# One written order of instructions replaced by another in a fused linear-attention and gated feed-forward kernel

## The chip, the cores and the metric

The kernel runs on one core of a Trainium2 chip. The metric is the device time of one execution in microseconds (us). The core has five engines that run side by side, each working through its own list of instructions in order: TensorE (PE, matrix products), VectorE (DVE), ScalarE (ACT), GpSimd (POOL) and SyncE (SP, which here only issues transfers by DMA). They wait for each other through semaphores.

## The reference

```python
q_s = exp(q - max(q, -1)); q_s /= sum(q_s, -1) + 1e-9      # softmax over the 64 head features
k_s = exp(k - max(k, 2));  k_s /= sum(k_s, 2) + 1e-9       # softmax over the 576 positions
kv  = einsum('bhsd,bhse->bhde', k_s, v)                    # one 64x64 matrix per head
x   = einsum('bhsd,bhde->bhse', q_s, kv)                   # 8 batches, 8 heads, 576 positions
x   = x.transpose(0, 2, 1, 3).reshape(4608, 512)
h   = x @ w_in                                             # 512 -> 2048
out = (h / (1 + exp(-beta * h))) @ w_out                   # 2048 -> 512, float32
```

All inputs and the output are float32; matrix operands are bfloat16 in the kernel.

## The kernel before, in words

The 4608 tokens are worked in nine chunks of 512: chunks 0 to 6 and 8 are the first 512 tokens of batches 0 to 7, and chunk 7 collects the last 64 tokens of every batch (`TAILS`). Each chunk goes through 16 steps `u`, one for every 128 of the 2048 hidden features. Steps are numbered through, `n = 16 * chunk + u`, 144 in all.

- `h n` (`st1`, L861): four matmuls of 512 columns, one for each of four contraction tiles, make `h` in one of four PSUM banks (`hT`). For `n` below 4 a step is cut into halves of 256 tokens and again into two parts of two contraction tiles (`h n half part`).
- `th n` (`tanh`, L879, ACT): tanh of `beta * h`, read from the bank.
- `g n` (`gate`, L896, DVE): `(th + 1) * h`, in bfloat16, one of 12 buffers. It frees the bank. The factor one half is put into the kv matrices.
- `o n` (`st2`, L927, and L919 in the last chunk): four matmuls add the step to four PSUM accumulators (`acc`). `oev` copies an accumulator to SBUF after 16 steps, `st` stores it.

Ahead of a chunk, its batch goes through the attention. `qmax`, `qsub`, `qexp`, `qsum`, `qrcp`, `qnorm` make the softmax of q; `kmax`, `kred`, `ksmall`, `krep`, `ksub`, `kexp` that of k; `vcast` turns v into bfloat16; `kv` (L617) and `kvn` (L636 to L639) make the kv matrices; `qtr` with its copy `qtrev` (batches 0 and 1, on PE), or `qT` (later batches, a transposing DMA issued by SP, L442), turn q; `x` (L667) multiplies, and `xev` copies `x` to the buffer `xT` in bfloat16, from which `h` reads. `xt` and `xtev` do that for the last 64 tokens. In batch 0 the pieces are smaller: `xev b jp half` (`x_ev_half`) writes the contraction tiles `jp` and `jp + 2` for one half of the chunk's tokens, a strided write. `kswap 0` (L495) exchanges key maxima between partitions by a matmul; `beta tr` (L342) transposes beta.

Loads are `ld q`, `ld k`, `ld v` (two for each batch, 576 KB each), `ld w` (16 parts of the two weights, 512 KB each, into four staging buffers) and `ld beta`. `cast w` turns a part into bfloat16. Batch `b` loads into the buffer of batch `b - 2`, so a load can stand behind the work of that batch. Eight semaphores serve SP's transfers in turn, so a transfer is issued once the one eight places before it has landed. `fill` are matmuls on constants that give PE something to do in the head.

What sets the order is the text `ORDER` at the top of the file (L17): a list of 1212 operations, written out by hand or by a planner outside the file. The last lines of the kernel go through it and issue each operation's instructions, in that order, to its engine; a word after `=` names the engine of an operation that has a choice:

```python
with tc.manual_schedule():
    for name, _, e in plan:
        fn, eng = ops[name]
        eng = e or eng
        fn(ENGINES[eng]) if eng else fn()
```

No engine changes its order at run time. The four `hT` banks are dealt out by the order too (`take`: the bank that has been free for the longest in the list), and so are the transfer semaphores. Waits are derived from the tiles and the ranges in them that the instructions touch.

Of the kernel before, what the change touches and what calls it, by code (L numbers as in the profile page):

```python
# [42 lines left out]
h_16_1, g_17, qmax_2_1, ld_w7_0, ld_k2_0, cast_w7_0=act, th_16, g_16, ld_q3_0, ld_v2_1, h_18, h_19, th_20, kmax_2_1,
th_18, o_12, g_20, g_18, qsub_2_0=pool, kmax_2_0, th_19, kred_2, g_19, qexp_2_3, ld_w7_1, h_23, th_23, qexp_2_1,
h_22, qexp_2_2, o_13, h_21, g_23, h_24, cast_w7_1=pool, o_14, ksmall_2, o_15, qexp_2_0, krep_2, th_21, ksub_2_0=pool,
g_21, qsum_2_2, th_22, g_22, qsum_2_3, vcast_2_1=act, qsum_2_1, oev_0_2=dve, oev_0_1=act, h_25, th_24, ld_v3_1,
ld_k3_0, g_24, qrcp_2_1, oev_0_0=act, oev_0_3=act, h_26, th_26, h_27, th_25, g_25, o_16, h_28, ld_v2_0, h_29, o_17,
kexp_2_0, ld_q4_0, ld_q3_1, qmax_3_1, ksub_2_1=pool, g_26, kexp_2_2, qmax_3_2, kexp_2_1, qnorm_2_1=pool, qsum_2_0,
o_18, o_19, vcast_3_1=act, th_28, ld_k3_1, st_0_3, qrcp_2_0, g_28, th_27, g_27, o_20, th_29, ld_v4_1, g_29, kmax_3_0,
ld_q4_1, qmax_3_0, kexp_2_3, vcast_2_0=pool, kv_2_0, kv_2_1, xt_0, xtev_0_0=act, ld_k4_0, o_21, xtev_0_1=dve,  # L50
qnorm_2_0=pool, qsub_3_0=pool, o_22, qexp_3_1, h_31, th_31, h_30, qexp_3_0, th_30, qmax_3_3, kmax_3_1, kmax_3_3,
o_23, o_24, kvn_2, o_25, o_26, qsub_3_1=pool, g_31, qexp_3_2, kmax_3_2, g_30, kred_3, qsum_3_2, qT_2, x_2_0,
# [981 lines left out]
```

## Time and profile before

| | us |
|---|---|
| median of three runs | 288.36 (288.12 to 288.61) |
| the profiled execution | 289.07 |
| its span, first to last instruction | 287.3 |
| PE busy | 277.1 |
| DVE busy | 202.1 |
| ACT busy | 175.3 |
| POOL busy | 127.9 |

The page is of one execution and reads like this: a row of a timeline has the start, the length, the engine, the line, the instruction, what it writes and reads, the number of instructions merged into the row, and in brackets how long the engine had been idle and what ended that. A matmul's shown length is that of a pipelined instruction: four matmuls of 512 columns that follow each other take about 0.86 us, less than their lengths together. Idle time of an engine that does not set the pace costs nothing.

### The profile page before, as it was taken

To read this page: it belongs to the slowest core of one execution; us is meant where nothing else is said; L and a number is where in the kernel's file an instruction comes from. 1 tells how busy PE (TensorE), PEld (TensorE's weight loads), DVE (VectorE), ACT (ScalarE), POOL (GpSimd) and SP (SyncE) were. 2 spreads that over 40 slices of the span, in tenths; PEclk is the share of its full clock that TensorE was granted. 3 is DMA by queue.
4 is the path that set the end of the run, shared out by engine and by line. 5 is a ranking of instruction groups with operands and counts; after the bars stand their busy time and mean duration, and the time that the engine had idled before them with its cause. 6 is when DMAs were issued, how large, how long until landed. Compare 5 with 4: busy or idle time off the path is not lost.

```text
span 287.3 us, 5186 instructions
## 1 busy us (share of the span) xinstructions
PE 277.1 (96%) x1969; PEld 128.9 (45%) x1969; DVE 202.1 (70%) x413; ACT 175.3 (61%) x302; POOL 127.9 (45%) x90
## 2 busy tenths in 40 slices
PE   7689999999999999999999999999999999999994
PEld 3255444444444444444444444444444444444542
DVE  3889967999999889999888747544664354536330
ACT  4878795995779577666875446436643454334422
POOL 5699895588398993367963620430020000000000
PEclk9899999999999999999999999999999999999999
DMA  7999999888966899950032930800025003000404
GB/s 254 385 392 387 387 387 390 321 294 267 256 178 228 188 341 390 280 169 1 0 96 108 209 149 1 228 2 0 2 66 165 0 3 145 0 0 1 148 0 146
DMA packets 36808, 50.01 MB, mean 174 GB/s; under 512 B 15648, under 2 KB 15920, under 8 KB 36784
## 3 DMA queue, kind: packets, MB, share of 16 engines
q1 hardware_dynamic: 36640, 49.56, 52.7%
q8 instruction: 15, 0.25, 0.4%
q10 hardware_dynamic: 144, 0.13, 0.1%
...
## 4 chain that ended last, share of the span: by engine, by line
PE 85%; DVE 5%; DMA 3%; POOL 2%; ACT 1%; issue 1%; SPq 1%; ACTq 0%
PE acc L927 40%; PE hT L861 40%; DMA beta_rows<-in_moe_beta_dram 3%; POOL kf L543 2%; PE hT L617 2%; DVE g L896 1%; PE hT L667 1%; SPq L273 1%; DVE km L478 1%; DVE kf L543 1%; PE hT L919 1%; PE acc L919 1%; DVE qs L420 1%; ACT th L879 1%; ACT xT L230 1%
## 5 line engine op out<-in xcount | busy, mean ns | idle before, releaser
L879 ACT ACTIVATE th<-hT,beta_c 128x512 bf16<-128x512 f32 (+1 forms) x148 | 95.3, 676 | 72.8 <-PE hT L861 54.5
L896 DVE SCALAR_TENSOR_TENSOR g<-th,hT 128x512 bf16<-128x512 bf16 x144 | 94.4, 678 | 56.5 <-ACT th L879 47.2
L927 PE MATMUL acc<-w_out_b,g 128*128 128x512 bf16 x560 | 133.7, 379 | 0.1
L861 PE MATMUL hT<-xT,w_in_b 128*128 128x512 bf16 (+1 forms) x528 | 119.0, 372 | 1.2 <-ACT xT L230 1.2
L861 PEld LDWEIGHTS <-w_in_b 128*128 128x128 bf16 x592 | 57.6, 98 | 67.5 <-DVE xT L232 1.4
L927 PEld LDWEIGHTS <-g 128*128 128x128 bf16 x560 | 53.5, 98 | 63.8 <-issue 3.1
L435 POOL TENSOR_TENSOR qn<-eq,qz 128x1152 bf16<-128x1152 bf16 (+2 forms) x20 | 34.7, 1739 | 54.7 <-DVE qz L427 34.2
L543 POOL TENSOR_TENSOR kf<-kf,kmb 128x1152 f32<-128x1152 f32 (+1 forms) x15 | 38.0, 2544 | 12.6 <-issue 5.3
L390 POOL TENSOR_TENSOR qf<-qf,qm 128x1152 f32<-128x1152 f32 (+2 forms) x19 | 33.4, 1769 | 15.0 <-DVE qm L374 11.5
L374 DVE TENSOR_REDUCE qm<-qf 128x9 f32<-128x576 f32 (+3 forms) x35 | 23.4, 690 | 4.7 <-DMA qf<-in_q_dram 4.6
L420 DVE TENSOR_REDUCE qs<-eq 128x9 f32<-128x576 bf16 (+2 forms) x33 | 23.0, 706 | 3.0 <-ACT eq L397 3.0
L478 DVE TRANSPOSE_TENSOR_REDUCE km<-kf 128x18 f32<-128x576 f32 (+1 forms) x30 | 23.4, 798 | 0.1
L397 ACT ACTIVATE eq<-qf 128x576 bf16<-128x576 f32 (+2 forms) x33 | 21.1, 654 | 3.2 <-POOL qf L390 3.0
L591 ACT ACTIVATE ek<-kf 128x576 bf16<-128x576 f32 x32 | 20.6, 681 | 0.9 <-DVE kf L543 0.6
L230 ACT CAST xT<-hT 128x512 bf16<-128x512 f32 x18 | 12.2, 739 | 14.7 <-PE hT L667 14.7
L861 PE MATMUL hT<-xTt,w_in_b 128*128 128x512 bf16 x64 | 14.6, 379 | 0.0
L363 PE MATMUL hT<-g,warm 128*128 128x512 bf16 x26 | 9.0, 492 | 1.5 <-POOL g L238 1.5
L232 POOL CAST va<-vf 128x1152 bf16<-128x1152 f32 x8 | 9.2, 1150 | 2.3 <-PE hT L617 2.3
L230 ACT CAST va<-vf 128x1152 bf16<-128x1152 f32 (+1 forms) x10 | 9.4, 961 | 0.6 <-DMA vf<-in_v_dram 0.6
L232 DVE CAST xT<-hT 128x512 bf16<-128x512 f32 x10 | 6.7, 726 | 4.1 <-PE hT L667 4.0
L232 DVE COPY osb<-acc 128x512 f32<-128x512 f32 x9 | 6.0, 684 | 3.1 <-PE acc L927 3.1
L230 ACT COPY osb<-acc 128x512 f32<-128x512 f32 (+1 forms) x11 | 6.1, 570 | 3.3 <-PE acc L927 2.3
...
## 6 DMA issues: line engine op xcount, KB each, us to landing
qf<-in_q_dram SPq DMA_DIRECT2D x16, 576.0 KB, 5.7
kf<-in_k_dram SPq DMA_DIRECT2D x16, 576.0 KB, 6.6
vf<-in_v_dram SPq DMA_DIRECT2D x16, 576.0 KB, 8.3
...
```

The costliest lines, as they stand in the source:

```text
L230: act.copy(dst, src)
L232: eng.tensor_copy(dst, src)
L374: dve.tensor_reduce(qm[:, j : j + n, i0:i1], qf[b % 2][:, j : j + n, i0:i1], axis=AX.X, op=ALU.max, negate=negate,)
L390: eng.tensor_tensor(x, x, m, ALU.subtract)
L420: dve.tensor_reduce(qs[:, i0:i1, j : j + n, 0:1], eq[:, i0:i1, j : j + n, :], axis=AX.X, op=ALU.add)
L435: eng.tensor_tensor(qn[b % 2][:, i0:i1, j : j + n, :], eq[:, i0:i1, j : j + n, :], z, ALU.mult)
L478: dve.tensor_reduce(km[:, j : j + n].rearrange("p j i e -> p (j i e)"), kf[b % 2][:, j : j + n].rearrange("p j i (e c) -> p (j i e) c", c=32),
L543: eng.tensor_tensor(x, x, m, ALU.subtract)
L861: pe.matmul(w, w_in_b[:, kt, u * P : (u + 1) * P], x[:, kt, cols(h)], start=(kt == 0), stop=(kt == KT - 1),)
L879: act.activation(th[turn(n, h) % 3][:, c], bank(n, h), ACTF.Tanh, scale=beta_c[:, u : u + 1])
L896: dve.scalar_tensor_tensor(out=out, in0=of, scalar=1.0, in1=src, op0=ALU.add, op1=ALU.mult)
L927: pe.matmul(acc[t][:], g[n % NG][:, t * P : (t + 1) * P], w_out_b[:, u, :], start=(u == 0), stop=(u == NJ - 1),)
```

## The change

The text `ORDER` is replaced as a whole. The operations are the same 1212, and so is the code below the list. Their sequence changes on all engines and in the loads, and 60 operations name another engine: 30 copies and casts go from DVE to ACT, 13 from ACT to DVE, 9 from POOL to ACT and 8 from ACT to POOL. The list is one line shorter, so lines below it have numbers smaller by one. The core of the diff, with the head, the stretch to the first steps of chunk 1, and the end:

```diff
-consts, ld_q0_1, qmax_0_0_j3, qexp_0_0_j3, qmax_0_1_1, qmax_0_0_j2, qmax_0_2_1, qsub_0_1_1=pool, qexp_0_1_1, ld_q0_0,
-ld_k0_1, ld_k0_0, ld_v0_1, ld_beta, qmax_0_2_0, qmax_0_1_0, qmax_0_0_0, qsum_0_1_1, ld_v0_0, kmax_0_1, qexp_0_0_j2,
-qsub_0_0_0=pool, qexp_0_0_0, qsum_0_0_0, qrcp_0_0, qsub_0_1_0=pool, qsub_0_2_1=pool, qsub_0_2_0=pool, qexp_0_1_0,
-qexp_0_2_0, ld_q1_0, qexp_0_2_1, vcast_0_j2=act, kmax_0_0, kred_0, fill_0, fill_5, fill_6, fill_10, fill_4, fill_2,
-ld_w0_0, fill_3, qnorm_0_0_1=pool, vcast_0_j3=act, ld_w0_1, qsum_0_1_0, beta_tr, fill_15, qnorm_0_0_0=pool, fill_7,
-qtr_0_0_1, ld_q1_1, kswap_0, fill_8, fill_1, fill_13, ld_w2_1, beta_ev, ksmall_0, krep_0_1, krep_0_0, vcast_0_j1=act,
-ld_w2_0, ksub_0_2=dve, fill_9, fill_16, ksub_0_3=pool, qrcp_0_1, ksub_0_0=dve, qsum_0_2_1, vcast_0_j0=act,
-qtrev_0_0_1=act, ld_w1_0, qnorm_0_1_0=pool, fill_11, ksub_0_1=dve, kexp_0_2, qnorm_0_1_1=pool, kexp_0_3, kexp_0_0,
-kexp_0_1, fill_12, qtr_0_0_0, kv_0_1, qtr_0_1_0, qtrev_0_1_0=act, qtrev_0_0_0=act, cast_w0_0_1=act, ld_w1_1,
-cast_w0_0_0=pool, cast_w0_1_1=pool, cast_w0_1_0=act, qmax_1_0, kv_0_0, fill_14, qmax_1_1, kvn_0, qtr_0_1_1, x_0_0_1,
-x_0_0_0, xev_0_0_0=act, qtrev_0_1_1=dve, x_0_1_1, x_0_1_0, qsum_0_2_0, ld_w4_0, xev_0_0_1=dve, h_0_0_0,
-qsub_1_0=pool, h_0_0_1, h_1_0_0, h_1_0_1, qrcp_0_2, ld_k1_1, xev_0_1_1=act, ld_w4_1, ld_k1_0, qnorm_0_2_0=pool,
-xev_0_1_0=dve, qmax_1_2, qmax_1_3, qnorm_0_2_1=pool, cast_w2_1=pool, th_0_0, h_2_0_0, qexp_1_1, h_2_0_1, qsum_1_1,
...
-cast_w4_0=pool, h_8, kmax_1_2, qrcp_1_1, qnorm_1_1=pool, qtrev_1_0=act, g_5, g_7, h_10, h_11, th_8, kmax_1_0,
-kmax_1_1, g_8, th_10, th_11, h_9, kred_1, ld_w3_1, ksmall_1, krep_1, cast_w3_0=pool, th_9, cast_w6_1=pool, ld_v1_0,
-ksub_1_0=pool, cast_w6_0=act, qtr_1_1, o_4, g_10, o_5, h_13, ksub_1_1=pool, g_11, cast_w3_1=act, ld_w5_0,
-cast_w5_0=pool, ld_v1_1, ld_w5_1, ld_q2_1, h_12, qtrev_1_1=dve, g_9, th_13, g_13, h_14, h_15, o_6, vcast_1_1=pool,
-o_7, o_8, ld_q2_0, cast_w5_1=pool, kexp_1_1, vcast_1_0=act, th_12, th_14, kexp_1_0, g_12, g_14, ld_k2_1, kv_1_0,
...
-o_143_1, oev_8_1=dve, st_7_3, o_137_3_1, o_138_3_1, o_139_3_1, st_8_0, o_138_3_0, o_139_3_0, o_140_3_0, o_141_3_0,
-o_142_3_0, o_143_3_0, oev_8_2=act, st_8_2, o_140_3_1, o_141_3_1, o_142_3_1, o_143_3_1, oev_8_3_0=act, st_8_1,
-st_8_3_0, oev_8_3_1=act, st_8_3_1
+consts, ld_q0_0, ld_q0_1, qmax_0_2_0, ld_k0_1, qsub_0_2_0=pool, qmax_0_0_0, qmax_0_1_0, qsub_0_0_0=pool, qexp_0_0_0,
+qmax_0_0_j3, qmax_0_0_j2, qmax_0_1_1, qexp_0_0_j3, qsum_0_0_0, qexp_0_0_j2, kmax_0_1, ld_k0_0, kmax_0_0, qrcp_0_0,
+fill_0, fill_1, fill_13, fill_15, fill_6, kred_0, fill_16, fill_12, qsub_0_1_1=pool, qsub_0_1_0=pool, ld_v0_1,
+qexp_0_1_1, qsum_0_1_1, ld_v0_0, vcast_0_j3=act, ld_beta, fill_2, fill_11, kswap_0, ksmall_0, qexp_0_1_0,
+vcast_0_j2=act, qnorm_0_0_1=pool, ld_q1_1, ld_w0_1, beta_tr, fill_7, qmax_0_2_1, qsub_0_2_1=pool, vcast_0_j0=act,
+vcast_0_j1=act, beta_ev, qexp_0_2_1, krep_0_0, krep_0_1, ksub_0_2=dve, kexp_0_2, ksub_0_3=pool, kexp_0_3, qsum_0_1_0,
+fill_4, qnorm_0_0_0=pool, ksub_0_0=dve, qrcp_0_1, qnorm_0_1_0=pool, kexp_0_0, ksub_0_1=dve, kexp_0_1, fill_5,
+fill_14, fill_10, qtr_0_0_1, fill_3, ld_w0_0, qnorm_0_1_1=pool, qtrev_0_0_1=act, qmax_1_3, fill_9, qmax_1_2,
+qexp_0_2_0, qtr_0_0_0, qtrev_0_0_0=act, kv_0_1, cast_w0_1_1=pool, cast_w0_0_1=pool, ld_w2_0, kv_0_0, ld_q1_0,
+ld_w2_1, qtr_0_1_0, cast_w2_0=pool, kvn_0, qtr_0_1_1, qtrev_0_1_0=dve, x_0_0_1, x_0_0_0, fill_8, xev_0_0_0=dve,
+qsum_0_2_1, qsum_0_2_0, qrcp_0_2, cast_w0_0_0=act, cast_w0_1_0=act, qtrev_0_1_1=act, x_0_1_1, x_0_1_0, xev_0_1_1=dve,
+ld_w1_0, xev_0_0_1=act, qsub_1_1=pool, ld_w1_1, qnorm_0_2_0=pool, h_0_0_0, h_2_0_0, h_0_0_1, h_2_0_1, h_1_0_0,
+cast_w2_1=pool, xev_0_1_0=act, h_1_0_1, h_3_0_0, th_0_0, ld_w4_0, th_1_0, ld_w4_1, h_0_1_0, h_0_1_1, qmax_1_0,
...
+cast_w4_1=act, qtrtev_0_0=act, o_3_0, qsum_1_0, qnorm_1_1=pool, ld_w6_1, h_8, qsum_1_1, qtrtev_0_1=act, g_7,
+qrcp_1_0, th_8, kmax_1_1, qnorm_1_0=pool, kmax_1_0, qtr_1_1, qtrev_1_1=act, h_10, ld_w3_1, h_9, cast_w6_0=pool, h_11,
+cast_w3_0=act, o_4, th_10, kmax_1_2, o_5, kmax_1_3, kred_1, ksmall_1, krep_1, ksub_1_1=pool, g_8, th_9, qtr_1_0,
+g_10, g_9, ld_w5_0, qtrev_1_0=dve, ld_v1_1, cast_w6_1=act, h_15, ksub_1_0=pool, vcast_1_1=pool, cast_w3_1=act, h_12,
+ld_v1_0, vcast_1_0=pool, o_6, o_7, h_14, th_11, th_12, ld_w5_1, kexp_1_2, cast_w5_0=act, g_11, h_13, g_12, kexp_1_3,
+th_15, g_15, o_8, kexp_1_1, o_9, ld_w7_0, kexp_1_0, kv_1_0, kv_1_1, cast_w5_1=pool, o_10, th_13, g_13, th_14, o_11,
...
+ld_q3_0, ld_v3_1, kmax_3_0, vcast_2_0=act, ld_k3_1, g_25, qrcp_2_1, qmax_3_0, h_29, kmax_3_2, ld_q4_0,
+vcast_3_1=pool, h_28, o_19, o_20, o_21, o_22, o_23, ld_k4_1, qnorm_2_1=pool, kexp_2_0, qmax_3_1, kexp_2_1, ld_k4_0,
+th_28, g_28, th_29, g_29, th_27, g_27, kmax_3_1, qmax_3_2, qmax_3_3, xt_0, xtev_0_1=act, kv_2_0, kv_2_1, kmax_3_3,
+o_24, qnorm_2_0=pool, xtev_0_0=act, qT_2, qsub_3_0=pool, qexp_3_1, kvn_2, qmax_4_0, kred_3, ksmall_3, ld_q4_1, h_30,
+h_31, th_30, th_31, g_31, o_25, o_26, g_30, o_27, o_28, ld_v4_0, x_2_1, qexp_3_0, x_2_0, qsub_3_1=pool, qexp_3_2,
...
+o_143_1, oev_8_1=act, st_8_0, st_8_1, o_138_3_0, o_138_3_1, o_139_3_0, o_140_3_0, o_141_3_0, o_139_3_1, o_142_3_0,
+o_143_3_0, oev_8_3_0=dve, st_8_3_0, o_140_3_1, o_141_3_1, o_142_3_1, o_143_3_1, oev_8_3_1=act, st_8_3_1
```

More of the change, by code (lines that the diff above doesn't have):

```diff
@@ L43 @@
[L43 to L52, printed above, removed]
@@ new lines @@
+ld_q5_0, qsum_3_0, qsum_3_1, xev_2_1=act, o_31, qtrt_1, oev_1_2=act, qtrtev_1_0=act, oev_1_3=act, qtrtev_1_1=dve,
+qmax_4_1, h_34, oev_1_0=act, th_34, ksub_3_0=pool, kmax_4_1, g_34, ksub_3_1=pool, h_33, th_33, g_33, qrcp_3_1,
+qnorm_3_1=pool, oev_1_1=act, h_32, th_32, g_32, qmax_4_2, h_37, qmax_4_3, th_37, qsub_4_1=pool, ld_v4_1,
+vcast_3_0=pool, h_35, qsub_4_0=pool, g_37, kmax_4_0, h_36, o_32, vcast_4_1=pool, h_39, o_33, h_38, o_34, ld_q5_1,
+kexp_3_3, th_35, qrcp_3_0, g_35, th_36, g_36, h_40, kexp_3_1, kexp_3_2, qmax_5_2, kexp_3_0, kred_4, h_43, ksmall_4,
@@ new lines @@
+kexp_4_1, ld_q6_0, ld_k6_1, xt_2, kmax_5_3, qnorm_4_1=pool, qexp_5_3, qexp_5_2, ld_q7_1, g_46, ld_q6_1, st_1_3,
+xtev_2_0=act, xtev_2_1=act, ld_v6_1, x_3_0, kmax_5_1, kred_5, xev_3_1=act, o_46, xev_3_0=dve, qsum_4_1, ld_v5_1,
+x_3_1, kv_4_0, kv_4_1, qmax_5_1, xev_3_2=act, kvn_4, o_47, ksmall_5, krep_5, xev_3_3=act, h_49, th_49, g_49, h_50,
+th_50, oev_2_0=act, h_48, g_50, th_48, g_48, h_53, oev_2_3=dve, th_53, qsub_5_0=pool, oev_2_2=act, h_56, g_53,
+qrcp_4_0, h_52, th_52, g_52, oev_2_1=dve, th_56, h_59, h_55, h_51, th_51, g_56, ksub_5_1=pool, qnorm_4_0=pool,
@@ new lines @@
+oev_3_1=act, st_2_3, st_3_1, ld_k7_1, h_76, th_74, o_64, g_74, kexp_5_1, h_75, qexp_6_0, th_73, th_75, o_65,
+qsum_6_0, g_73, qrcp_6_0, g_75, h_78, qexp_7_3, th_76, th_78, g_76, qsum_7_3, kexp_6_2, h_77, o_66, ld_k7_0, o_67,
+o_68, qnorm_6_0=pool, xt_4, g_78, th_77, g_77, xtev_4_1=dve, xtev_4_0=act, st_2_1, kv_5_0, kv_5_1, xt_3,
+xtev_3_1=act, o_69, o_70, h_79, o_71, o_72, o_73, o_74, xtev_3_0=act, qexp_7_2, kexp_6_1, kmax_7_2, th_79, st_3_0,
+kvn_5, g_79, qT_5, st_2_2, qmax_7_1, qT_6, o_75, qmax_7_0, qsum_7_2, x_5_0, x_5_1, xev_5_0=dve, kmax_7_1,
```

117 lines of the change are left out of this document (53 added, 64 removed).

## The prediction, written before the result

> **What bounds the kernel now.** I read the page's engine shares and slices first, then a table by stage, what TensorE (PE) waited for after the head, and the timelines of the head. The page and the stage table:
>
> ```profile
> PE 277.1 (96%) x1969; PEld 128.9 (45%) x1969; DVE 202.1 (70%) x413; ACT 175.3 (61%) x302; POOL 127.9 (45%) x90
> L879 ACT ACTIVATE th<-hT,beta_c 128x512 bf16<-128x512 f32 (+1 forms) x148 | 95.3, 676 | 72.8 <-PE hT L861 54.5
> vf<-in_v_dram SPq DMA_DIRECT2D x16, 576.0 KB, 8.3
> ...
> 10.00:20.00 10.00, 8.15 (x120) 4.38 (x119) 8.78 (x24) 8.62 (x18) 8.21 (x10) 0.83 1.05 390
> 24.00:42.00 18.00, 18.00 (x104) 9.07 (x102) 15.70 (x33) 15.59 (x27) 15.65 (x10) 1.00 1.05 387
> 50.00:100.00 50.00, 50.00 (x399) 23.07 (x398) 47.07 (x104) 39.84 (x68) 38.63 (x20) 1.00 0.82 249
> ...
> PE hT L861 <- ACT xT L230: 1.2, 2, 0.7
> ```
>
> The columns of the table are the window, its length, and the busy time of PE, weight loads, DVE, ACT and POOL, then clock and DMA. In the stream PE is busy without a break (18.00 of 18, 50.00 of 50), although DVE is 94% busy between 50 and 100 us. The last row, of PE's waits after 20 us, is the only one there: two waits for `xT`, both in the head. So the kernel is a head of some 22.5 us in which PE waits, and then about 261 us of PE work at full rate. The change keeps every matmul; the PE list also keeps 15 separate groups of small attention matmuls after the head, as before. Hence only three things can move the time: when the feed-forward matmuls really get going, stalls that open or close in the stream, and the tail.
>
> **The head, before.** Timelines of PE, DVE and ACT (start, length, engine, line):
>
> ```profile
> 11.74 0.23 PE L342 MATMUL hT<-ident_f,beta_rows 16*128 16x16 f32 x1 [0.64 <-DMA beta_rows<-in_moe_beta_dram]
> 13.16 0.54 PE L495 MATMUL hT<-kmr,swap 128*128 128x8 f32 x2
> 13.93 1.06 PE L363 MATMUL hT<-eq,warm 128*128 128x512 bf16 x2
> 14.79 1.45 PE L363 MATMUL hT<-g,warm 128*128 128x512 bf16 x5
> 17.86 0.48 PE L617 MATMUL hT<-va,ek 64*64 64x65 bf16 x34 [0.32 <-ACT ek L591]
> 19.27 0.94 PE L667 MATMUL acc<-qT,kvn 64*64 64x256 bf16 x16 [0.39 <-DVE kvn L639]
> 20.69 1.14 PE L861 MATMUL hT<-xT,w_in_b 128*128 128x256 bf16 x9 [0.48 <-ACT xT L230]
> 22.54 0.71 PE L861 MATMUL hT<-xT,w_in_b 128*128 128x256 bf16 x5 [0.71 <-ACT xT L230]
> ...
> 10.80 1.32 DVE L478 TRANSPOSE_TENSOR_REDUCE km<-kf 128x36 f32<-128x1152 f32 x1
> 12.16 0.23 DVE L489 TENSOR_REDUCE kmr<-km 128x8 f32<-128x72 f32 x1
> 13.74 0.16 DVE L518 TENSOR_TENSOR kmx<-kmr,hT 128x8 f32<-128x8 f32 x1 [0.76 <-PE hT L495]
> 16.34 0.74 DVE L543 TENSOR_TENSOR kf<-kf,acc 128x576 f32<-128x576 f32 x1
> 18.92 0.49 DVE L639 TENSOR_TENSOR kvn<-hT,kz 128x128 bf16<-128x128 f32 x2
> 19.32 0.41 DVE L232 COPY qT<-acc 128x512 bf16<-128x512 bf16 x1
> 19.66 0.28 DVE L420 TENSOR_REDUCE qs<-eq 128x2 f32<-128x128 bf16 x1
> 20.00 0.73 DVE L232 CAST xT<-acc 128x512 bf16<-128x512 f32 x1
> 20.63 0.14 DVE L426 TENSOR_REDUCE qz<-qs 128x4 f32<-128x8 f32 x1
> 20.81 0.18 DVE L427 RECIPROCAL qz<-qz 128x4 f32<-128x4 f32 x1
> 21.72 0.73 DVE L232 CAST xT<-acc 128x512 bf16<-128x512 f32 x1 [0.73 <-PE hT L861]
> ...
> 15.86 1.94 ACT L591 ACTIVATE ek<-kf 128x576 bf16<-128x576 f32 x3
> 19.90 0.74 ACT L230 CAST xT<-acc 128x512 bf16<-128x512 f32 x1
> 21.76 0.73 ACT L230 CAST xT<-acc 128x512 bf16<-128x512 f32 x1 [1.12 <-PE hT L861]
> ```
>
> Four copies bring `xT` from PSUM for the first chunk: two for the first half of the tokens (19.90, 20.00) and two for the second (21.72, 21.76). The second pair needs no result of the `h` matmuls, yet it waited for them, and the `h` matmuls then waited for the pair until 22.54: a hole of 0.87 us after the ninth matmul (20.69 + 8 x 0.109 + 0.11 = 21.67). The program tracks `xT` by the range that a strided write spans, so a write for contraction tiles 1 and 3 also stands in the way of tile 2, and a later write waits for earlier reads.
>
> **Step 1: until `x 0` starts.** It loses one delay. The swap matmul (13.16) no longer stands behind transposes and a fill; and `kmax 0 0` (10.80) no longer stands behind a sum and a reciprocal. The key maximum `kmx` comes at about 12.5 instead of 13.74 (`kmax 0 0` at 9.8, one microsecond earlier, 1.32, the reciprocal pair 0.45, `kred` 0.23, then 0.58 from the swap matmul to `kmx` as in 13.16 to 13.74, and 0.1 of hand-over). DVE then has an extra sum, a maximum and the same subtractions, so the last key subtraction ends near 16.6 instead of 17.08. It gains another: the beta load is issued after both v loads instead of one: 576 KB more at the 390 GB/s of the stage table, or 1.5 us, so the beta transpose waits on PE until about 13.2. Behind it stand six fills at the slow pace of the head (0.43 us each by the row of 13.93), a transpose, three more fills and a transpose: `kv 0` then starts at about 17.4 and ends near 18.3, as it did at 17.86 + 0.48. So `x 0` starts at 19.25, as before (19.27). Bounds: 18.7, if only the last key exponential (16.6 + 0.68) sets `kv 0`, and 19.6, if the slow pace lasts through all nine fills.
>
> **Step 2: from `x 0` to a running `h` stream.** In the new list all of `x 0`, and both `xev 0 0 1` (ACT) and `xev 0 1 1` (DVE), stand ahead of `h 0 0 0`. By the semaphores in the built program its first matmul waits for `xev 0 0 0`, its second for `xev 0 1 1` too, by the same range. On DVE the line is: `qtrev 0 1 0`, `xev 0 0 0`, two sums, the reduction and reciprocal of `qrcp 0 2`, then `xev 0 1 1`. The first copy starts 0.7 after `x 0`, at 19.95, and ends at 20.69; the sums take 0.2 each start to start, `qrcp` 0.35; `xev 0 1 1` runs 21.3 to 22.05. The second `h` matmul starts at 22.1 and nine run to `h 1 0 0`, the last at 22.1 + 8 x 0.109 = 22.97. `xev 0 1 0` (ACT), now last, waits for that one, as the pair of 21.72 did, 0.27 after its start, takes 0.73, and `h 1 0 1` goes at 24.04. Before, PE went on at 22.54 with nine done; now at 24.04 with ten: 1.50 - 0.11 = **+1.4 us**. With the bounds of step 1: +0.85 to +1.75.
>
> **Step 3: the stretch to 50 us.** PE, DVE and POOL rows:
>
> ```profile
> 53.97 1.73 PE hT L861 x8
> 41.69 3.03 PE L927 MATMUL acc<-w_out_b,g 128*128 128x512 bf16 x12
> ...
> 29.70 1.41 DVE L420 TENSOR_REDUCE qs<-eq 128x9 f32<-128x576 bf16 x2
> 32.74 1.22 DVE L896 SCALAR_TENSOR_TENSOR g<-th,hT 128x512 bf16<-128x512 bf16 x2
> 37.30 1.25 DVE L896 SCALAR_TENSOR_TENSOR g<-th,hT 128x512 bf16<-128x512 bf16 x2
> ...
> 42.62 1.03 POOL L232 CAST w_out_b<-wst 128x1024 bf16<-128x1024 f32 x1
> ```
>
> Before, DVE spreads the key maxima of batch 1 between gates; from 29.70 to 37.30 it does two sums, a reciprocal, four maxima with their reduction, and three gates in 7.6 us. Now `g 8` stands behind four sums, two reciprocals, two gates and all of the maxima: 7.6 + 1.4 + 0.4 - 0.6 + 0.65 for itself = 9.45 us after `g 4`, which ends at 29.85 (the 22 remaining half steps of `h` end at 24.04 + 22 x 0.109 = 26.4, two steps take 1.73, tanh and gate about 0.7 each with 0.3 of hand-over). That is 39.3. PE reaches `qtr 1 0`, which takes the bank that `g 8` frees, after 14 steps of 0.863 (row of 53.97; eight half steps counted as four) and 0.7 of transposes, from 26.4: 39.2. Then `h 15` waits for `g 10` in the same way. I take +0.3; bounds 0 and +0.8. A stall goes: the twelve matmuls of 41.69 take 3.03 instead of 2.75, because half of a `w_out` block, needed by `o 8`, was cast on POOL only from 42.62, behind the key subtractions. In the new list ACT casts that half: -0.28, bounds 0 and -0.28.
>
> **Step 4: middle and tail.** Of the copies, 17 fewer run on DVE and 18 more on ACT; both have room while PE has none, so 0 (bounds -0.2 and +1.0, the upper from the DVE-laden 50 to 100 us). The end:
>
> ```profile
> 283.13 0.37 ACT L230 COPY osb<-acc 128x256 f32<-128x256 f32 x1 [1.04 <-PE acc L919]
> 283.57 0.37 ACT L230 COPY osb<-hT 128x256 f32<-128x256 f32 x1
> 283.97 0.65 ACTq L961 DMA_DIRECT2D out_dram<-osb  x1
> ```
>
> The last half is still one 0.37 copy on ACT behind the last matmul and one store; the half before it goes to DVE. 0, bounds +-0.2. **Sum:** 1.4 + 0.3 - 0.28 = +1.4 on the profiled execution's 289.07 us, 290.5; that execution lies 0.7 over the median of 288.36, so the median comes to **289.8 us**.
>
> **Rivals.** *The clock falls back* (slower still). The stage table shows 0.83 between 10 and 20 us, with fills at 0.43 us each, double the 0.216 of the stream. In the new head PE has about 1.2 us of work between 18.7 and 22.1. If the clock halves there, it would stay so for some 3.3 us, as from the row of 11.74 into that of 14.79, whose five fills are only partly slow: +1.7, 291.5 us. Against it: before, a similar gap around 20 us left it at 1.00. [...]
> *A transpose by DMA comes late.* `x 2` needs `qT 2`, 4.8 us from issue by the page:
>
> ```profile
> qT<-qn SPq DMA_TRANSPOSE x6, 4.8
> L435 POOL TENSOR_TENSOR qn<-eq,qz 128x1152 bf16<-128x1152 bf16 (+2 forms) x20 | 34.7, 1739 | 54.7 <-DVE qz L427 34.2
> ```
>
> If `qnorm 2 0` starts only with `o 24`, it takes about 2.1 and the transpose 4.8; PE has seven steps, 6.0 us: a stall of 0.9, 290.7 us. Against: POOL idled 34 us waiting for DVE, so it ran ahead of need.
> *The hole closes* (faster). If `h 0 0 0` did not wait for `xev 0 1 1` and `xev 0 1 0` came in time, the 0.87 hole and the 0.28 stall go: 287.2 us. For it: three of the four copies now stand ahead of `h`. Against it: the semaphores. It decides if the second `h` matmul starts before about 20.7 and PE goes on without a stop.
> *Nothing moves*: PE's full stream hides all, because step 1 gains what step 2 loses (`x 0` before 18.3): 288.4.
>
> **How the numbers follow.** Forecast (+0.6 to +2.6) 0.53; clock 0.15; late transpose or another stall of that kind 0.12; nothing 0.08; hole closes 0.12. So slower 0.80, same 0.08, faster 0.12, with 0.2% (0.58 us) about what runs from 288.12 to 288.61 can tell. The range leaves out the closed hole and a clock loss on top of the upper bounds: 288.0 to 291.9; the forecast's own is 289.0 to 291.0.
>
> **What would show it.** Right: the first `h` matmul near 20.7, alone, a wait of over a microsecond for a DVE copy of `xT`, a second hole of about 1 us before 24.1, beta's transpose near 13.2, and a short PE wait near 39 us for a gate. Step 1 is wrong if `x 0` starts before 18.7; step 2 if `h` runs through; step 3 if PE shows no wait between 35 and 45 us; step 4 if PE is under full anywhere after 50 us. The prediction is wrong if the last matmul ends within half a microsecond of 283.5.

## The result, and the profile after

The changed kernel takes 291.42 us, the median of nine runs from 289.53 to 292.95; beside it, on the same chip, the kernel before took 288.12 us (nine runs, 287.93 to 289.61). The ratio is 1.0094, with a 95% interval of 1.007 to 1.0119: slower by 3.3 us. The forecast was slower, 289.8 us in a range from 288.0 to 291.9: the sign and the range held, and the size of the loss was twice what was forecast. The runs of the changed kernel also lie 3.4 us apart, those of the kernel before 1.7.

The profiled execution took 291.42 us with a span of 289.5. First the page: engine shares, the slices of PE and of its clock, and PE's group of the `h` matmuls, the one that waits for `xT`.

```profile
PE 275.4 (95%) x1939; PEld 129.7 (45%) x1969; DVE 192.6 (67%) x396; ACT 182.4 (63%) x320; POOL 127.5 (44%) x89
...
PE   7587999999999999999999999999999999999994
...
PEclk9869999999999999999999999999999999999999
...
L860 PE MATMUL hT<-xT,w_in_b 128*128 128x512 bf16 (+1 forms) x519 | 117.7, 372 | 2.6 <-DVE xT L231 1.4
```

Seen in slices of 7.2 us, PE is below full only in the first four and the last, and its clock is below nine tenths only in the second and third, between 7 and 22 us (line numbers are smaller by one than before). The 1939 matmuls are records: 30 of the kernel's 1969 are missing from this trace, so that PE's sum is a little short. DVE lost 9.5 us of work and ACT gained 7.1, as the list says, and neither shows in the time. The head in PE's timeline (start, length, engine, line, operation, and in brackets the idle time before it and what ended it):

```profile
11.69 0.36 PE L494 MATMUL hT<-kmr,swap 128*128 128x8 f32 x2 [1.03 <-DVE kmr L488]
13.05 0.28 PE L341 MATMUL hT<-ident_f,beta_rows 16*128 16x16 f32 x1 [1.01 <-DMA beta_rows<-in_moe_beta_dram]
...
18.07 1.18 PE L616 MATMUL hT<-va,ek 64*64 64x65 bf16 x72
...
20.19 0.60 PE L666 MATMUL acc<-qT,kvn 64*64 64x256 bf16 x8 [0.39 <-DVE kvn L638]
...
21.69 0.27 PE L860 MATMUL hT<-xT,w_in_b 128*128 128x256 bf16 x1 [0.23 <-DVE xT L231]
23.08 1.16 PE L860 MATMUL hT<-xT,w_in_b 128*128 128x256 bf16 x9 [1.13 <-DVE xT L231]
25.06 3.21 PE L860 MATMUL hT<-xT,w_in_b 128*128 128x256 bf16 x25 [0.82 <-ACT xT L229]
```

The reader sees three stops: one microsecond for the beta rows ahead of 13.05 (the kernel before waited 0.64 us for them, ahead of 11.74), and the two waits for `xT` of 1.13 and 0.82 us after a single `h` matmul. `x 0` starts at 20.19 (before: 19.27), and `h` runs from 25.06 (before: from 22.54, with one matmul fewer done). The copies they wait for, on DVE and ACT:

```profile
12.08 0.16 DVE L517 TENSOR_TENSOR kmx<-kmr,hT 128x8 f32<-128x8 f32 x1
...
15.09 0.69 DVE L542 TENSOR_TENSOR kf<-kf,acc 128x576 f32<-128x576 f32 x1
...
20.90 0.74 DVE L231 CAST xT<-acc 128x512 bf16<-128x512 f32 x1 [0.23 <-PE acc L666]
21.53 0.46 DVE L419 TENSOR_REDUCE qs<-eq 128x2 f32<-128x128 bf16 x2
...
22.31 0.71 DVE L231 CAST xT<-acc 128x512 bf16<-128x512 f32 x1
...
20.86 0.74 ACT L229 CAST xT<-acc 128x512 bf16<-128x512 f32 x1 [0.44 <-PE acc L666]
24.28 0.73 ACT L229 CAST xT<-acc 128x512 bf16<-128x512 f32 x1 [2.68 <-PE hT L860]
```

The second DVE copy (22.31) stands behind the two sums and the reciprocal, and the second ACT copy waited 2.68 us until an `h` matmul whose data it does not touch was through.

The table by stage, cut here where the granted clock changes (window, its length, busy time of PE, weight loads, DVE, ACT and POOL with their counts, clock, DMA). The changed kernel:

```profile
8.84:12.26 3.42, 1.19 (x6) 0.49 (x4) 3.26 (x8) 2.51 (x9) 1.23 (x2) 1.00 1.05 398
12.26:15.67 3.41, 2.62 (x7) 1.06 (x8) 3.38 (x9) 3.41 (x9) 3.41 (x5) 0.50 1.02 367
15.67:19.08 3.41, 3.41 (x84) 2.25 (x82) 1.43 (x3) 2.62 (x7) 3.41 (x5) 0.50 1.05 399
19.08:22.49 3.41, 2.01 (x41) 1.09 (x32) 2.75 (x12) 1.62 (x3) 2.96 (x2) 1.00 1.07 391
```

and the kernel before:

```profile
8.36:11.77 3.41, 1.21 (x5) 0.35 (x4) 3.27 (x5) 2.48 (x8) 2.90 (x5) 1.00 1.05 400
11.77:15.18 3.41, 3.41 (x13) 1.75 (x14) 2.55 (x8) 2.71 (x6) 2.24 (x3) 0.50 1.03 375
15.18:18.60 3.42, 3.10 (x88) 1.99 (x87) 3.35 (x10) 3.31 (x6) 3.31 (x5) 1.00 1.05 400
18.60:22.01 3.41, 2.36 (x30) 1.36 (x27) 2.50 (x11) 2.19 (x5) 3.29 (x5) 1.00 1.06 389
```

In both profiles the granted clock changes at the edges of windows of 3.41 us: to 0.50 at 11.77 and back at 15.18 before, to 0.50 at 12.26 and back at 19.08, two windows later, now. Both kernels enter a window in which PE works 1.2 us (1.21 before, 1.19 now), and the clock is 0.50 in the next. Before, the wait for beta was over when that slow window began; PE was busy through the window (3.41), and a clock of 1.00 followed. Now PE stands still for 0.8 us of it, waiting for beta, and a second slow window follows, to 19.08. In it fills, transposes and most of the 72 `kv` matmuls (1.18 us) run at a clock of 0.50.

After 25.06 the stream is as it was. The waits of PE from 24 to 60 us, in one view, hold a single line, the last wait for `xT`:

```profile
PE hT L860 <- ACT xT L229: 0.8, 1, 0.8
```

From the point where `h` runs to the end of the span it is 289.5 - 25.06 = 264.4 us, and before 287.3 - 22.54 = 264.8 with one matmul (0.11) more: the long rest of the new order costs nothing. So the spans differ by 2.2 us: 2.5 that `h` runs later, less 0.11, less 0.2 in the rest. The medians differ by 3.3, because the profiled execution of the kernel before is one of its slower ones (289.07 us).

### The profile page after: what moved, and what is told of

Its sections match the earlier page's. It is cut to its first block, busy times and chain, and to the rows that moved or that the text cites. A ratio compares the mean times of both kernels' runs of the same rounds, so it can differ in the third digit from the quotient of the medians.

```text
span 289.5 us, 5142 instructions
## 1 busy us (share of the span) xinstructions
PE 275.4 (95%) x1939; PEld 129.7 (45%) x1969; DVE 192.6 (67%) x396; ACT 182.4 (63%) x320; POOL 127.5 (44%) x89
## 4 chain that ended last, share of the span: by engine, by line
PE 92%; DMA 3%; issue 1%; SPq 1%; DVE 1%; ACT 1%; DVEq 0%
PE hT L860 43%; PE acc L926 42%; DMA beta_rows<-in_moe_beta_dram 3%; PE hT L616 2%; PE hT L362 1%; PE hT L666 1%; SPq L272 1%; PE hT L918 1%; PE acc L918 1%; DVE xT L231 1%; PE hT L457 0%; PE hT L708 0%; PE acc L457 0%; ACT xT L229 0%; PE acc L666 0%
## 5 line engine op out<-in xcount | busy, mean ns | idle before, releaser
L926 PE MATMUL acc<-w_out_b,g 128*128 128x512 bf16 x540 | 130.1, 379 | 1.9 <-issue 1.3
L860 PE MATMUL hT<-xT,w_in_b 128*128 128x512 bf16 (+1 forms) x519 | 117.7, 372 | 2.6 <-DVE xT L231 1.4
L229 ACT CAST xT<-hT 128x512 bf16<-128x512 f32 x21 | 13.9, 741 | 13.2 <-PE hT L666 13.2
L229 ACT CAST xTt<-hT 128x128 bf16<-128x128 f32 x11 | 2.8, 307 | 13.4 <-PE hT L708 13.4
L231 POOL CAST va<-vf 128x1152 bf16<-128x1152 f32 x9 | 10.3, 1151 | 0.0
L229 ACT COPY osb<-acc 128x512 f32<-128x512 f32 x15 | 8.4, 590 | 2.3 <-PE acc L926 2.2
L229 ACT CAST va<-vf 128x1152 bf16<-128x1152 f32 (+1 forms) x9 | 8.3, 940 | 0.9 <-DMA vf<-in_v_dram 0.9
L362 PEld LDWEIGHTS <-warm 128*128 128x128 bf16 x34 | 4.0, 122 | 9.0 <-issue 6.8
```

What stands on the lines that cost most here:

```text
L229: act.copy(dst, src)
L860: pe.matmul(w, w_in_b[:, kt, u * P : (u + 1) * P], x[:, kt, cols(h)], start=(kt == 0), stop=(kt == KT - 1),)
L926: pe.matmul(acc[t][:], g[n % NG][:, t * P : (t + 1) * P], w_out_b[:, u, :], start=(u == 0), stop=(u == NJ - 1),)
```

## The experiments

The theory after the comparison: the head holds the whole loss, as (a) two false waits for `xT`, and (b) half-clock windows, which the late beta load lengthens and which come into the `h` stream because PE does little in the hole. The rival: the remaining order, or the late copies themselves. All kernels, six to twelve runs each, with the ratio to the kernel before timed beside them on the same chip (288.12 us beside the changed kernel, and 288.33, 288.21 and 288.18 us beside the others, which were timed in three sets):

| kernel | median us | range | ratio to before, 95% interval |
|---|---|---|---|
| changed kernel | 291.42 | 289.53 to 292.95 | 1.0094, 1.007 to 1.0119 |
| e1_beta | 290.77 | 289.66 to 292.29 | 1.0084, 1.006 to 1.0107 |
| e1b_fills | 290.96 | 289.68 to 292.67 | 1.0082, 1.0051 to 1.0112 |
| e2_ranges | 288.21 | 287.53 to 289.14 | 0.9992, 0.998 to 1.0005 |
| h_before_head | 288.80 | 288.36 to 289.07 | 1.001, 1.0 to 1.002 |
| e4_hole_filled | 291.60 | 290.26 to 292.66 | 1.0113, 1.0086 to 1.0141 |
| e6_before_ranges | 287.46 | 287.14 to 289.21 | 0.9975, 0.9959 to 0.9992 |
| h_after_head | 290.92 | 290.43 to 292.27 | 1.0093, 1.0071 to 1.0115 |
| e3_beta_ranges | 287.53 | 286.93 to 288.53 | 0.9975, 0.996 to 0.9989 |
| e4b_hole_filled | 290.36 | 289.81 to 290.75 | 1.0067, 1.005 to 1.0084 |
| e8_head_filled | 291.12 | 289.30 to 292.29 | 1.009, 1.0058 to 1.0121 |
| e9_all | 287.34 | 286.90 to 288.40 | 0.9965, 0.9949 to 0.9981 |
| e10_before_all | 287.31 | 287.18 to 289.80 | 0.997, 0.9951 to 0.999 |

**e2_ranges: the false waits taken away.** The order is the changed kernel's; only the place of the first chunk's data in `xT` changes.

```diff
-        x = xT[b % 2][:].rearrange("p (J c) (t n i) -> p c J t i n", c=2, i=2, n=64)
+        x = first_x()[:, h, jp].rearrange("p J (t n i) -> p J t i n", i=2, n=64)
...
-        cast(eng, x[:, jp, :, 2 * h : 2 * h + 2], w)
+        cast(eng, x, w)
...
+    def first_x():
+        flat = xT[0][:].rearrange("p k c -> p (k c)")
+        return flat.rearrange("p (h j J c) -> p h j J c", h=2, j=2, J=2)
+
+    def first_part(kt, h):
+        x = first_x()[:, :, kt % 2, kt // 2]
+        return x if h is None else x[:, h]
...
-                x[:, kt, cols(h)],
+                x[:, kt, cols(h)] if c else first_part(kt, h),
```

> The changed kernel with the first chunk's xT stored as (token half, pair of tiles, tile, token), so that every one of the four copies writes one unbroken range and no h matmul waits for a copy whose data it does not read. The order is the same. Theory (the two waits for xT after the first h matmul are false, and all of their time is on the path): the first h matmul stays at 21.7, the h stream is unbroken or waits less than 0.3 us, its 32 half steps end near 25.3 instead of 27.5, and the time falls by 1.5 to 2.2 us, to 289.2 to 289.9 us. Rival (the copies are late in truth, or a later wait takes up the gain): a fall below 0.6 us, the wait reappearing behind a copy, a tanh or a w block.

Measured: 288.21 us, 3.2 less than the changed kernel. PE's timeline:

```profile
13.20 0.28 PE L342 MATMUL hT<-ident_f,beta_rows 16*128 16x16 f32 x1 [0.91 <-DMA beta_rows<-in_moe_beta_dram]
...
20.23 0.60 PE L667 MATMUL acc<-qT,kvn 64*64 64x256 bf16 x8 [0.40 <-DVE kvn L639]
...
21.73 7.18 PE L869 MATMUL hT<-xT,w_in_b 128*128 128x256 bf16 x48 [0.23 <-DVE xT L232]
```

This execution has the same two slow windows (to 18.94) and `x 0` at the same place as the changed kernel's profile, and 48 `h` matmuls now run from 21.73 without a stop. It took 289.14 us, the profiled one of the changed kernel 291.42: 2.28 us, the length of the two waits with their starting gaps (25.06 - 21.69 less ten matmuls of 0.11 is 2.27). Both waits were false and wholly on the path. The medians say about 1 us more than that (3.2); where it comes from is the question of the filled holes below.

**e6_before_ranges: the same in the kernel before.** The diff is that of e2_ranges, on the kernel before.

> The kernel before, order unchanged, with the first chunk's xT stored as (token half, pair of tiles, tile, token), so that each copy writes one unbroken range. Theory (the hole of 0.87 us behind the ninth h matmul is a false wait on the path): h runs on without a stop, 0.7 to 0.9 us less, 287.4 to 287.7 us. Rival (the copies of the second half come too late by themselves, or a later wait takes the gain): 288.0 us or more.

Measured 287.46 us, 0.75 less than before (0.87 is the hole's length). The timeline shows `h` in one piece:

```profile
18.95 0.94 PE L667 MATMUL acc<-qT,kvn 64*64 64x256 bf16 x16 [0.39 <-DVE kvn L639]
20.36 7.22 PE L869 MATMUL hT<-xT,w_in_b 128*128 128x256 bf16 x48 [0.48 <-ACT xT L230]
```

With the ranges in both orders (e2 and e6) 0.75 us of the 3.3 remain, or 0.6 when each is set against the kernel before timed beside it.

**e1_beta: the beta load early again.**

```diff
-qexp_0_1_1, qsum_0_1_1, ld_v0_0, vcast_0_j3=act, ld_beta, fill_2, fill_11, kswap_0, ksmall_0, qexp_0_1_0,
+qexp_0_1_1, qsum_0_1_1, ld_beta, ld_v0_0, vcast_0_j3=act, fill_2, fill_11, kswap_0, ksmall_0, qexp_0_1_0,
```

> The changed kernel with one load moved: ld_beta goes ahead of the second v load, its place in the kernel before. Theory (the head costs it, part of it through the clock): the beta transpose starts near 11.7 us instead of 13.05, TensorE no longer idles from 12.05 to 13.05, the clock is released after one window of 3.4 us as in the kernel before, x 0 starts near 19.2 instead of 20.19, and the time falls by 0.9 to 1.7 us, to 289.7 to 290.5 us, with runs closer together than 289.5 to 293. The hole of 25 us stays. Rival (the rest of the order costs it, or the clock's second window has another cause): within 0.4 us of 291.4.

Measured 290.77: 0.65 less than the changed kernel, less than expected, and the intervals of the two overlap. The spread hardly shrank (2.6 us). The profiled execution, 291.31 us, tells why. Its timeline and its clock windows:

```profile
12.17 0.23 PE L342 MATMUL hT<-ident_f,beta_rows 16*128 16x16 f32 x1
...
18.36 0.60 PE L667 MATMUL acc<-qT,kvn 64*64 64x256 bf16 x8 [0.33 <-ACT w_in_b L230]
...
23.22 7.03 PE L861 MATMUL hT<-xT,w_in_b 128*128 128x256 bf16 x35 [0.82 <-ACT xT L230]
```

```profile
20.11:23.53 3.42, 1.48 (x13) 1.18 (x13) 2.29 (x6) 0.73 (x1) 3.42 (x4) 1.00 1.05 385
23.53:26.94 3.41, 3.41 (x18) 2.43 (x17) 0.69 (x1) 2.12 (x6) 3.41 (x4) 0.50 1.05 388
```

`h` runs 1.84 us earlier than in the changed kernel's profile (23.22 against 25.06), yet the span is only 0.3 us shorter (289.2). The clock was 1.00 from 16.70 to 23.53, but PE did only 1.48 us of work in the window of the hole, and the next 3.41 us, all in the `h` stream, were granted 0.50: by that about 1.7 us lost where nothing hides it.

**e1b_fills: the idle microsecond filled, beta still late.**

```diff
-vcast_0_j2=act, qnorm_0_0_1=pool, ld_q1_1, ld_w0_1, beta_tr, fill_7, qmax_0_2_1, qsub_0_2_1=pool, vcast_0_j0=act,
+vcast_0_j2=act, qnorm_0_0_1=pool, ld_q1_1, ld_w0_1, fill_7, fill_5, fill_14, fill_10, beta_tr, qmax_0_2_1,
```

> The changed kernel with four fills (7, 5, 14, 10) moved ahead of the beta transpose, so that TensorE works where it idled from 12.05 to 13.05 us; the load of beta stays late. Theory (the idle microsecond keeps the clock at half for a second window): the gap is filled, one slow window instead of two, x 0 near 19.3, time 289.7 to 290.5 us. Rival (the lateness of beta itself costs, through the chain behind it, whatever the clock does): two slow windows as in the changed kernel, or x 0 still near 20.2, within 0.4 us of 291.4.

Measured 290.96, which tells nothing apart from e1_beta or the changed kernel; its profiled execution (292.55 us) has a mean clock of 0.982, which is about three windows of 3.41 us at half in 290.8, and nine `h` matmuls from 21.54 take 2.10 us (1.16 in e1_beta). Inconclusive.

**e3_beta_ranges: beta early and the ranges.** The diffs of e1_beta and e2_ranges together.

> The changed kernel with both edits: beta's load ahead of the second v load, and the first chunk's xT in unbroken ranges. With the ranges alone the median was 288.2 us, with beta alone 290.8 us. Theory (beta's lateness leaves TensorE idle from 12.05 to 13.05 us, so that a half-clock window in the head is not followed by a release, and x 0 comes at 20.2 us instead of 18.4): x 0 between 18.4 and 19.3 us in the profile, median 287.4 to 287.9 us. Rival (beta's place does not matter, its run differed by the phase of the clock's windows alone): 288.2 us within 0.3.

Measured 287.53, 0.68 less than e2_ranges, as e1_beta was 0.65 below the changed kernel. The windows of its profile lie within 0.1 us of those of e2_ranges, so the two can be set side by side. First e2_ranges, then e3_beta_ranges:

```profile
8.71:12.12 3.41, 1.13 (x6) 0.43 (x4) 3.25 (x6) 2.24 (x10) 0.96 (x2) 1.00 1.04 403
12.12:15.53 3.41, 2.50 (x9) 0.99 (x9) 3.38 (x11) 3.41 (x8) 3.41 (x4) 0.50 1.04 361
15.53:18.94 3.41, 3.41 (x65) 2.11 (x67) 1.81 (x3) 2.69 (x7) 3.41 (x5) 0.50 1.05 403
```

```profile
8.79:12.20 3.41, 0.86 (x4) 0.28 (x3) 3.25 (x6) 1.86 (x8) 0.75 (x2) 1.00 1.05 402
12.20:15.61 3.41, 3.38 (x10) 1.46 (x11) 3.27 (x10) 3.41 (x9) 3.38 (x4) 0.50 1.01 356
15.61:19.02 3.41, 3.21 (x100) 2.15 (x98) 3.24 (x10) 3.41 (x9) 3.41 (x5) 1.00 1.05 402
```

Both have a slow window from 12.1 or 12.2 us. With beta late PE works 2.50 us in it, and the next window is at 0.50 too; with beta early it works 3.38, and the next is at 1.00. `x 0` starts at 20.23 in the one and at 18.63 in the other. The price of a late beta is a longer slow stretch, in those executions whose windows lie so. Where no slow window comes ahead of `x 0`, the late load costs it nothing that shows: in the profile of h_after_head (below; mean clock 0.998), with the changed kernel's own head, two fills at 13.31 take 0.59 us, where two at 13.67 take 1.06 in the changed kernel's profile, and `x 0` starts at 18.09; in that of e1_beta, with beta early and two fills at 12.55 also in 0.59, it starts at 18.36. In the median the price is about 0.7 us, by two comparisons of the same sign; in each the two intervals overlap.

**e4_hole_filled: idle matmuls in the hole.**

```diff
-    FILLS = [(14, None)] + [(2, (h, J)) for h in range(2) for J in range(2)] + 12 * [(1, None)]
+    FILLS = [(14, None)] + [(2, (h, J)) for h in range(2) for J in range(2)] + 12 * [(1, None)] + [(6, None), (4, None)]
...
-xev_0_0_1=act, qsub_1_1=pool, ld_w1_1, qnorm_0_2_0=pool, h_0_0_0, h_2_0_0, h_0_0_1, h_2_0_1, h_1_0_0,
+xev_0_0_1=act, qsub_1_1=pool, ld_w1_1, qnorm_0_2_0=pool, fill_17, h_0_0_0, h_2_0_0, h_0_0_1, h_2_0_1, h_1_0_0, fill_18,
```

> The changed kernel with ten fills added where TensorE stands still between x 0 and the running h stream: six ahead of the first h matmul, four behind h 1 0 0. They do no work of the result and no copy waits for them; the two waits for xT stay as long as they are. Theory (the hole costs in two ways: its own length, +1.4 us over the kernel before, and a half-clock window of 3.4 us in the h stream behind it, which comes in some executions because TensorE did too little in the window of the hole): the h stream still resumes 5 us after x 0 starts, no half-clock window lies behind it, the slowest executions go, and the median falls by about 0.7 to 1.2 us, to 290.2 to 290.7 us. Rival (the half-clock windows come from the head ahead of x 0 alone, not from the hole): within 0.4 us of 291.4. Rival (only the hole's length counts): also within 0.4 us of 291.4, or slower if the fills delay something.

Measured 291.60: a miss. The two new fills took PSUM banks of their own, every later step got another bank, and PE waited for gates to free them:

```profile
PE hT L861 <- DVE g L896: 0.6, 2, 0.4
```

The run therefore mixes two things. It was made again without the change of banks.

**e4b_hole_filled.**

```diff
         w = bank(n, h)
+        for _ in range(12 if (n, h, ks[0]) == (0, 0, 0) else 0):
+            pe.matmul(w, warm[:], g[NG - 1][:, 0:256], start=True, stop=True)
         for kt in ks:
...
+        for _ in range(8 if (n, h, ks[0]) == (1, 0, 0) else 0):
+            pe.matmul(bank(0, 1), warm[:], g[NG - 1][:, 0:256], start=True, stop=True)
         if KT - 1 in ks:
```

> The changed kernel with idle matmuls in the hole, as in the run before, but into PSUM banks that the h matmuls own in any case, so that no later bank changes hands: twelve of 256 columns ahead of the first h matmul, eight behind h 1 0 0. Theory (about 1 us of the loss is half-clock windows in the h stream that the hole brings about): no wait for a gate follows, h resumes 4.9 us after x 0, the median falls by 0.6 to 1.0 us, to 290.4 to 290.8 us. Rival (the half-clock windows come from the part ahead of x 0): 291.4 us within 0.3.

Measured 290.36 us, 1.06 less than the changed kernel, and all six runs within 289.81 to 290.75. The timeline, with `h` no earlier after `x 0` than in the changed kernel (24.16 - 19.29 = 4.87; there 25.06 - 20.19 = 4.87), and the windows of hole and stream:

```profile
19.29 0.60 PE L666 MATMUL acc<-qT,kvn 64*64 64x256 bf16 x8 [0.40 <-DVE kvn L638]
...
20.49 1.48 PE L860 MATMUL hT<-g,warm 128*128 128x256 bf16 x12
...
24.16 6.09 PE L862 MATMUL hT<-xT,w_in_b 128*128 128x256 bf16 x37
```

```profile
20.99:24.40 3.41, 3.31 (x31) 2.62 (x29) 2.36 (x6) 0.73 (x1) 3.41 (x5) 1.00 1.05 383
24.40:27.81 3.41, 3.36 (x27) 2.51 (x26) 1.74 (x3) 3.17 (x9) 3.41 (x3) 1.00 1.06 391
```

The hole's length stays, 1.4 us more than before. Executions above 290.75 us, six of the changed kernel's nine, are gone. The intervals of the two kernels overlap (1.005 to 1.0084 against 1.007 to 1.0119), so the medians alone do not settle it; the granted clock of every run helps. One slow window takes about 0.006 off the mean clock of an execution (3.41 us at half, out of 289). Six of the changed kernel's nine runs had 0.982 to 0.988, by this estimate two or three slow windows, and these are the six slow ones. Here all six runs have 0.991 to 0.994, by the same estimate about one; with e2_ranges, which has the same list and head and no hole, two of twelve runs have 0.988 and the others 0.994. So the further slow windows come mostly with the hole, not from the part ahead of `x 0`, and matmuls that yield nothing make the kernel faster by keeping the clock up.

**e8_head_filled: idle matmuls ahead of `x 0` instead.**

```diff
+    FILLS[12] = FILLS[11] = (5, None)
...
         take("beta")
+        for _ in range(4):
+            pe.matmul(place["beta"], warm[:], g[NG - 1], start=True, stop=True)
```

> The changed kernel with twelve idle matmuls more ahead of x 0, in the three places where TensorE stands still between 8.9 and 13 us: four before the last query fill, four before the key swap, four before the beta transpose. The hole behind x 0 stays, and so does the place of beta's load. Theory (the part ahead of x 0 is late by the clock alone: a mostly idle window at 9 to 12 us halves it): full clock through to x 0, which starts near 18.2 us instead of 20.19, 289.4 to 290.0 us, with less spread. Rival (beta's late load or DVE sets x 0): x 0 stays above 19.5, 291.4 us within 0.4. If the extra matmuls meet a half-clock window, they delay the swap and the time rises.

Measured 291.12: the median missed, and the runs fall into two groups. Three took 289.30 to 289.68 us with a mean clock of 0.998 to 1.000, five took 291.07 to 292.29 with 0.988 to 0.994. The profiled execution (292.06) is of the second. Its `x 0` starts at 17.94, in line with the expectation, and then:

```profile
17.59:21.00 3.41, 1.47 (x20) 0.74 (x21) 3.11 (x10) 1.76 (x5) 3.41 (x4) 1.00 1.05 386
21.00:24.42 3.42, 2.60 (x13) 1.66 (x12) 1.06 (x2) 0.85 (x2) 3.42 (x5) 0.50 1.05 389
24.42:27.83 3.41, 3.41 (x17) 2.35 (x16) 0.84 (x2) 2.22 (x6) 3.41 (x4) 0.50 1.05 390
```

A window of 1.47 us of work around `x 0` and the first `h` matmul, and two at half clock behind it, the second wholly in the `h` stream. The three executions with a mean clock of 0.998 to 1.000 are at 289.3 to 289.7; in the profiled one the clock was 1.00 from 14.18 to 21.00, and the slow windows came back behind the hole alone.

**h_before_head and h_after_head: the two orders joined at the end of the half steps.** In the first the list begins as that of the kernel before, through `h_3_1_1`, and goes on with the operations that are left in the changed kernel's sequence; the second is the other way round.

```diff
-consts, ld_q0_0, ld_q0_1, qmax_0_2_0, ld_k0_1, qsub_0_2_0=pool, qmax_0_0_0, qmax_0_1_0, qsub_0_0_0=pool, qexp_0_0_0,
+consts, ld_q0_1, qmax_0_0_j3, qexp_0_0_j3, qmax_0_1_1, qmax_0_0_j2, qmax_0_2_1, qsub_0_1_1=pool, qexp_0_1_1, ld_q0_0,
...
```

> The order of the kernel before up to and with h 3 1 1, then the order of the changed kernel for all that is left. Theory (the head is all of the loss; the rest of the new order costs nothing): 288.1 us within 0.4. Rival (the middle or the tail of the new order costs): 289.0 us or more, up to 291.4. If the removed stall of 0.28 us near 42 us counts, 287.8.

> The order of the changed kernel up to and with h 3 1 1, then the order of the kernel before for all that is left. Theory (the head holds the whole loss): 291.4 us within 0.5, with the same spread as the changed kernel. Rival (the rest of the new order holds part of the loss): 290.5 us or less. The run with the two orders the other way round came to 288.8 us against 288.3, which leaves 0 to 0.6 us for the rest.

Measured 288.80 us for the head of before with the rest of the changed kernel: 0.47 us over the kernel before (0.1%), 0.3 above what was expected, and 2.6 us under the changed kernel. The head of the changed kernel with the rest of before took 290.92. This one has a new stop of its own at the seam, in the waits of PE:

```profile
PE hT L861 <- DVE g L896: 1.4, 1, 1.4
```

and clocks of 0.998 to 0.988, so that its figure is no measure of the head alone. The first of the two carries the verdict: the head holds at least 2.6 of the 3.3 us. What the other 0.5 us of h_before_head are is not shown; the rest of the changed kernel took no longer than that of the kernel before in their own profiles (264.4 against 264.8 us), so they may belong to the joining.

**e9_all and e10_before_all: both false waits away and the clock held up.** e9_all is e3_beta_ranges with nine more idle matmuls where PE stands still between 8.9 and 12 us, e10_before_all is e6_before_ranges with nine between 8 and 11.4 us. The lines added, first e9_all, then e10_before_all:

```diff
+    FILLS[12] = (5, None)
+    FILLS[11] = (6, None)
...
+    FILLS[2:5] = [(6, (0, 1)), (4, (1, 0)), (5, (1, 1))]
```

> The changed kernel with beta's load early, the first chunk's xT in unbroken ranges, and nine idle matmuls more where TensorE stands still between 8.9 and 12 us. Without these matmuls the median was 287.53 us, with one run at full clock at 286.93. Theory (the half-clock window in the head is what is left to win): full clock throughout, 286.9 to 287.1 us, faster than the kernel before by 0.4%. Rival (the half-clock window lies under other work): 287.5 us within 0.2.

> The kernel before with the first chunk's xT in unbroken ranges and nine idle matmuls more in the three places where TensorE stands still between 8 and 11.4 us. Without these matmuls the median was 287.46 us, four of its runs at full clock at 287.14 to 287.24 and one at 287.67. Theory: full clock in nearly all executions, 287.1 to 287.3 us. Rival: 287.46 us within 0.1, because one half-clock window in the head of this kernel costs nothing.

Measured 287.34 and 287.31 us: both faster than the kernel before by 0.3%, with intervals that exclude no change (the table). Against the same kernels without the idle matmuls it is 0.2 us, which these runs do not tell from nothing. Four executions of e9_all took 286.90 to 286.95 us. The profiled execution of e9_all, its slowest at 288.40 us, still has a mean clock of 0.994, about one slow window, and its two fills at 15.65 take 1.06 us where two at 12.54 take 0.59, so the nine matmuls do not keep full clock in every execution. The new order with the two repairs is as good as the old one with one.

## Why the prediction was right in sign and short in size

**Step 1 failed in its size.** It put `x 0` at 19.25, within 18.7 to 19.6; the profile has 20.19. What DVE does came even earlier than said (`kmx` at 12.08, forecast 12.5; the last key subtraction ends at 15.78, forecast 16.6), and the beta transpose stood at 13.05, forecast 13.2. The term that failed is "six fills at the slow pace ..., `kv 0` then starts at about 17.4": the upper bound let the slow pace last through nine fills, but it went on through the transposes and all of `kv 0`, because PE, waiting for beta, worked 2.62 us of the slow window from 12.26, and the clock was 0.50 in the next one too. The pair of e3_beta_ranges and e2_ranges shows this: 18.63 against 20.23. Worse, `x 0` is not one number: in the profiles of kernels that leave this head as it is, it starts at 18.09 (h_after_head, mean clock 0.998), 19.29 (e4b_hole_filled, one slow window ahead of it, from 14.16) and 20.19 to 20.46 (the changed kernel and e2_ranges, two slow windows, and e4_hole_filled, mean clock 0.986). This term explains the profiled execution: 290.5 was forecast for it, 291.42 came, and 0.94 of that is `x 0`.

**Step 2 was right.** The first `h` matmul stood alone, 1.50 us after `x 0` (forecast 1.45); the second waited for the DVE copy behind the two sums; the second hole followed; from the first matmul to the running stream it took 3.37 us, forecast 3.35. e2_ranges prices the two waits at 2.28 us; less the old hole of 0.87 (0.75 by e6_before_ranges) that is +1.4 to +1.5.

**The first rival came true in part.** "The clock falls back" named the place (little PE work behind `x 0`) and the price (1.7 us, 291.5 us in all), and was given a chance of 0.15. The profiles of e1_beta and e8_head_filled show just that fall, and e4b_hole_filled puts it at about 1.1 us in the median: it comes in part of the executions, and not in the profiled one of the changed kernel, whose clock is 1.00 from 19.08 on. The argument against it was that a similar gap at 20 us had left the clock at 1.00 in one profile. The gap was not so similar: its window (18.60 to 22.01) held 2.36 us of PE work, and the prediction counted on 1.2; and one execution was too few, since the windows lie elsewhere in each. The trust in a single profile is the error behind both misses. That 291.42 us lies within 288.0 to 291.9 is luck in part: the upper bound was made of waits, and what filled it was mostly the clock.

**Step 3 hardly shows.** A wait of 0.3 us near 39 us was forecast, as was that the stall of the `o` matmuls goes. PE's timeline:

```profile
35.51 0.62 PE L457 MATMUL hT<-ident,qn 128*128 128x128 bf16 x8
35.97 2.75 PE L860 MATMUL hT<-xT,w_in_b 128*128 128x512 bf16 x12
...
40.31 0.61 PE L457 MATMUL hT<-ident,qn 128*128 128x128 bf16 x8
40.91 1.89 PE L860 MATMUL hT<-xT,w_in_b 128*128 128x512 bf16 x8
42.63 1.89 PE L926 MATMUL acc<-w_out_b,g 128*128 128x512 bf16 x8
...
46.09 1.89 PE L926 MATMUL acc<-w_out_b,g 128*128 128x512 bf16 x8
```

The list of PE's waits from 36 to 46 us is empty, so by the prediction's own sign this step is wrong. What can be seen is that from the eight transposes of 40.31 to the next start, `h 15`, it takes 0.60 us, and from those of 35.51 only 0.46: about 0.14 us, where the forecast has `h 15` wait for `g 10`. The stall is gone: `o 8` and `o 9` are the eight of 46.09. Eight matmuls in 1.89 us is the full rate (40.91 to 42.63 are eight at 0.215). **Step 4 was right**: nothing lost in the middle or at the tail, 264.4 us from the running stream to the end against 264.8. **The other rivals**: no late transpose was seen; "the hole closes" and "nothing moves" are excluded by the profile.

The loss of 3.3 us, by the runs: 1.4 for the false waits, about 1.1 for the half-clock windows that the hole brings about, about 0.7 for beta's late load, 0.1 left over. The first is read from timelines. The last two are differences of medians whose intervals overlap, uncertain by 0.5 to 1.0 us, so that their sizes are rough and the small remainder says little; it was not tried whether they add up exactly.
